# A decode step with attention over a cached K and V: V in tiles of 8 heads in one buffer, K in halves, one softmax per pair

## The chip, the cores and the metric

The kernel runs on one core of a Trainium2 chip. The metric is the device time of one execution in microseconds (us), lower is better. The core has five engines that run side by side and meet at semaphores: PE (TensorE: matrix products, transposes), DVE (VectorE: elementwise work and sums along a row), ACT (ScalarE: activations and copies out of PSUM), POOL (GpSimd: small elementwise work) and SP (SyncE: it only issues transfers here). Transfers are carried by 16 DMA engines; SP's all go through one queue in the order of issue.

## The reference

Eight sequences have one new token each. The token is normalised, projected to 32 query heads of 128, and attends to 4096 cached keys per head; beside it runs a small MLP. The outputs are added.

```python
xn = _layernorm(x, axis=-1)                       # x: 8 x 1 x 640
q = (xn @ wq).reshape(B, 1, 32, 128)              # one query per head
scores = einsum("bhqd,bhkd->bhqk", q, k) * 128 ** -0.5     # k, v: 8 x 32 x 4096 x 128 bf16
p = softmax(scores, axis=-1)
o = einsum("bhqk,bhkd->bhqd", p, v)
return x + o.reshape(B, 1, 4096) @ wo + gelu(_layernorm(xn) @ w1 + b1) @ w2 + b2
```

The K and V caches are 256 MB each, and each of their elements is used once. All weights together are some 15 MB.

## The kernel before, in words

**Tiles.** A tile is 4 heads of one sequence: 4 x 4096 keys, laid out so that partition p holds 128 keys of head p // 32, one after another (32 KB a partition, 4 MB a tile). There are 64 tiles (`NQ`), index i. K and V have two tiles of buffer each (`K_sb`, `V_sb`, slot i % 2).

**Scores.** A tile's keys are split. The first 88 of each partition's 128 are done by DVE in four chunks (`dve_chunk`, L480): multiply by the query, which lies on every partition (`qbc_sb`), add the two halves of the row, sum the rest, into `Sd_sb`. The last 40 (`JP`) are done by PE in five banks of 8: `pe_T` (L437) transposes 8 keys into PSUM, `act_T` (L449) copies them to `KT_sb`, `pe_QK` (L457) multiplies them by the queries of all four heads, so that PSUM (`S_ps`) holds for each key a score against each of the four heads, of which one belongs to it. `act_S` (L470) picks that one with four copies, one for the 32 partitions of each head.

**Softmax.** `dve_max` (L499) finds the maximum over 32 partitions' scores with two 32x32 transposes and makes the bias; `act_exp` (L512) takes the exponential in four instructions of 32 partitions, one a head, each writing its own column of `P_sb` (the other columns stay zero, from one memset at the start) and its row sums. `pe_RS` and `dve_rinv` make the inverse of the sums.

**Output.** `pe_PV` (L535) multiplies V by `P_sb`, key row by key row: 128 products, each with four columns. The zeros keep the heads apart. `act_O` copies the result, `o_norm` (L554) scales it on POOL and spreads it for the last step. After all tiles, `pe_ox` / `cp_ox` turn it, and `fin_wo` multiplies by wo (160 products onto the sum that the MLP began).

**Queries.** `qrep` (POOL), `pe_qbc` and `act_qbc` put the next tile's query on all partitions.

**Order.** Each step is put at a position by `at(pos, fn, ...)` (L686 and on), with tile i at 100 i; the sorted list is then replayed to each engine in that order, so that an engine's order is fixed by hand. PE, DVE and ACT run tiles two by two in a loop of 32 rounds. SP replays its issues in order too: an issue that waits holds up those behind it. `load_k(i)` (L300) waits until tile i-2 has been transposed and multiplied, `load_v(i)` (L310) until PV of tile i-2 is done. The loads of wo come last.

**Start.** The weights of the MLP lie in the second slots of K_sb and V_sb; so K of tile 1 waits for the first MLP product (`mlp1`) and V of tile 1 for the second (`mlp`). The first slots are free at once.

The steps print with the line numbers of the kernel. The profile puts nearly all instructions on L104, where the recorded calls are replayed, so its groups are told apart by tile names; an operation that writes `KT_sb` from `TR_ps` is `act_T`.

Of the kernel before, what the change touches and what calls it, by code (L numbers as in the profile page):

```python
# [13 lines left out]
P = 128  # L14
# [132 lines left out]
def bass_parallel_sum__gqa_block_cached__mixer_channel_mlp__decode_kernel(  # L147
# [17 lines left out]
    HS = 4  # L165
    HP = P // HS
    NKEY = SK * HS // P
    NHQ = H // HS
    NQ = NHQ * B
# [6 lines left out]
    LOOP0, LOOPN = -0.1, 32  # L176
    PAD = 64
    VFIRST = 16
    NR = H * DH // P
    assert NKEY == 128  # L180
    NS = 5

    JP = 40

    def chunks(i):
        jd = NKEY - JP
        n = -(-jd // CHMAX)
        return [(jd * c // n, jd * (c + 1) // n) for c in range(n)]

    bank0 = [0]  # L190
    for i_ in range(NQ):
        bank0.append(bank0[-1] + JP // TPB)
    chunk0 = [0]
    for i_ in range(NQ):
        chunk0.append(chunk0[-1] + len(chunks(i_)))
    V_CUT = {}
    K_CUT = {}
    WO_CUT = (0, 16, 26, 30, NR)
    DQ = DH // NR

# [3 lines left out]
    with ExitStack() as es:  # L204
# [6 lines left out]
        V_sb = sb("V_sb", [P, 2, NKEY, DH], BF)  # L211
# [3 lines left out]
        M_sb = V_sb[:, 1, :, :].rearrange("p j d -> p (j d)")  # L215
        w2_sb = M_sb[:, 0:(FB + 1) * D].rearrange("p (c n) -> p c n", n=D)
        wo_sb = W_sb[:, 0:NR * D].rearrange("p (c n) -> p c n", n=D)
        assert DC * F <= NKEY * DH and (FB + 1) * D <= NKEY * DH and NR * D <= DC * H * DH
# [5 lines left out]
        Sd_sb = sb("Sd_sb", [P, 2, NKEY], F32)  # L224
        P_sb = sb("P_sb", [P, 2, NKEY, HS], BF)
        qT_sb = sb("qT_sb", [P, H, B], BF)
        qrep_sb = sb("qrep_sb", [P, 2, HS, HP], BF)
        qbc_sb = sb("qbc_sb", [P, 2, DH], BF)
        oN_sb = sb("oN_sb", [P, 2, HS], F32)
# [3 lines left out]
        oU_sb = sb("oU_sb", [P, 2, HS], F32)  # L233
# [14 lines left out]
        mq_sb = sb("mq_sb", [P, 1], F32)  # L248
        nsc_sb = sb("nsc_sb", [P, 32], F32)
        mb_sb = sb("mb_sb", [P, 32], F32)  # L250
        NB_sb = sb("NB_sb", [P, 2, 32], F32)
        rs4_sb = sb("rs4_sb", [P, 2, HS], F32)
        ri4_sb = sb("ri4_sb", [P, 2, HS], F32)
# [9 lines left out]
        TRF = TR_ps[:, :, :].bitcast(F32)  # L263
        TRB, SB_, PVB = [_Bank(), _Bank()], [_Bank(), _Bank()], [_Bank(), _Bank()]
        CHB, ACCB = _Bank(), _Bank()
        RS_ps = CH_ps[:, 0:2 * HS].rearrange("p (s h) -> p s h", h=HS)
        QT_ps = CH_ps[:, 64:64 + H * B]
        HT_ps = CH_ps[:, 64:64 + (FB + 1) * B]
        OX_ps = S_ps[:, 0, 0:B * NR].rearrange("p (b c) -> p b c", c=NR)

        pe, dve, act, sp, pool = (_Eng(sem(f"{n}_s")) for n in ("pe", "dve", "act", "sp", "pool"))
        NPIECE = 4
        ld_k = [[_Dma(sem(f"ld_k{s}_{q}")) for q in range(NPIECE)] for s in range(2)]
        ld_v = [[_Dma(sem(f"ld_v{s}_{q}")) for q in range(NPIECE)] for s in range(2)]
# [13 lines left out]
        def cuts(kind, i):  # L288
            c = (K_CUT if kind == "k" else V_CUT).get(i, (0, NKEY))
            return list(zip(c[:-1], c[1:]))  # L290

        def piece_of(kind, i, lo, hi):
            return [tk[(kind, i, q)] for q, (a, b) in enumerate(cuts(kind, i)) if a < hi and b > lo]

        def cache_src(cache, i, lo, hi):
            hq, b = divmod(i, B)
            return cache[b, hq * HS:(hq + 1) * HS].rearrange(
                "h (p j) d -> (h p) j d", j=NKEY)[:, lo:hi, :]

        def load_k(i):  # L300
            s = i % 2
            if i >= 2:
                sp.wait(tk[("kt", i - 2)], tk[("km", i - 2)])
            elif i == 1:
                sp.wait(tk["mlp1"])
            for q, (lo, hi) in enumerate(cuts("k", i)):
                tk[("k", i, q)] = ld_k[s][q].sig(sp.dma_start(
                    K_sb[:, s, lo:hi, :], cache_src(A_k_cache, i, lo, hi)))

        def load_v(i):  # L310
            s = i % 2
            if i >= 1:
                sp.wait(tk[("pv", i - 2)], tk["mlp"])
            for q, (lo, hi) in enumerate(cuts("v", i)):
                tk[("v", i, q)] = ld_v[s][q].sig(sp.dma_start(
                    V_sb[:, s, lo:hi, :], cache_src(A_v_cache, i, lo, hi)))

        def load_mlp():
            tk["w1"] = ld_w1.sig(sp.dma_start(w1_sb, B_w1.rearrange("(p c) f -> p c f", c=DC)))
            tk[("v", -1, 0)] = tk["w2a"] = ld_v[1][0].sig(sp.dma_start(  # L320
                w2_sb[:, 0:FB, :], B_w2[0:FB * P, :].rearrange("(p c) n -> p c n", c=FB)))
            sp.wait(tk["vz"])
            tk["w2b"] = ld_w2b.sig(sp.dma_start(w2_sb[0:FLAST, FB, :], B_w2[FB * P:F, :]))
# [7 lines left out]
        def consts_pool():  # L331
            tk["iota"] = pool.sig(pool.iota(iota_i[:, :], [[1, P]], base=0, channel_multiplier=-1))
            tk["vz"] = pool.sig(pool.memset(M_sb[:, FB * D:NKEY * DH], 0.0))
            pool.memset(Sd_sb[:, 1, :], 0.0)
# [3 lines left out]
            pool.memset(rs4_sb[:, :, :], 0.0)  # L338
# [3 lines left out]
            pool.wait(t)  # L342
            tk["pz"] = pool.sig(pool.memset(P_sb[:, :, :, :].rearrange("p n j h -> p (n j h)"), 0.0))
# [33 lines left out]

        def pe_xT(w):
# [32 lines left out]
        def qrep(i):  # L411
            hq, b = divmod(i % NQ, B)
            s = i % 2
            pool.wait(tk[("q", hq * HS)], tk.get(("qb_pe", i - 2)), tk.get(("qkl", i - 2)))
            tk[("qrep", i)] = pool.sig(pool.tensor_copy(
                qrep_sb[:, s, :, :],
                qT_sb[:, hq * HS:(hq + 1) * HS, b][:, :, None].to_broadcast([P, HS, HP])))

        def pe_qbc(i):
            k = trn[0] % 2  # L420
            trn[0] += 1
            pe.wait(tk[("qrep", i)], tk["id"])
            TRB[k].use(pe)
            tk[("qb_pe", i)] = TRB[k].used(pe, pe.sig(pe.matmul(
                TRF[:, k, 0:DH], qrep_sb[:, i % 2, :, :].rearrange("p h r -> p (h r)"),
                ident_bf[:, :], start=True, stop=True)))
            tk[("qbk", i)] = k

        def act_qbc(i):
            k = tk[("qbk", i)]  # L430
            act.wait(tk.get(("km", i - 2)))
            TRB[k].use(act)
            tk[("qb", i)] = TRB[k].used(act, act.sig(act.activation(
                qbc_sb[:, i % 2, :], TRF[:, k, 0:DH], ACT.Copy)))


        def pe_T(i, t):  # L437
            k = trn[0] % 2
            trn[0] += 1
            s = i % 2  # L440
            j0 = NKEY - JP + t * TPB
            pe.wait(tk["id"], piece_of("k", i, j0, j0 + TPB))
            TRB[k].use(pe)
            for jj in range(TPB):
                last = pe.transpose(TR_ps[:, k, jj * P:(jj + 1) * P], K_sb[:, s, j0 + jj, :], ident_bf[:, :])
            tk[("T", i, t)] = (k, TRB[k].used(pe, pe.sig(last)))
            tk[("kt", i)] = tk[("T", i, t)][1]

        def act_T(i, t):  # L449
            k, _ = tk[("T", i, t)]  # L450
            n = bank0[i] + t
            act.wait(tk.get(("qk", n - NS)))
            TRB[k].use(act)
            tk[("ev", n)] = TRB[k].used(act, act.sig(act.activation(
                KT_sb[:, n % NS, :, :].rearrange("p a b -> p (a b)"), TR_ps[:, k, :], ACT.Copy)))

        def pe_QK(i, t):  # L457
            n = bank0[i] + t
            s = i % 2
            pe.wait(tk[("ev", n)], tk[("qrep", i)])  # L460
            if t == 0:
                SB_[s].use(pe)
            for jj in range(TPB):
                c0 = (t * TPB + jj) * HS
                last = pe.matmul(S_ps[:, s, c0:c0 + HS], KT_sb[:, n % NS, jj, :],
                                 qrep_sb[:, s, :, 0], start=True, stop=True)
            tk[("qk", n)] = SB_[s].used(pe, pe.sig(last))
            tk[("qkl", i)] = tk[("qk", n)]

        def act_S(i):  # L470
            s = i % 2
            if i >= 2:
                act.wait(tk[("exp", i - 2)])
            SB_[s].use(act)
            for h in range(HS):
                r = slice(h * HP, (h + 1) * HP)
                last = act.activation(Sd_sb[r, s, NKEY - JP:NKEY], S_ps[r, s, h:JP * HS:HS], ACT.Copy)
            tk[("s", i)] = SB_[s].used(act, act.sig(last))

        def dve_chunk(i, c):  # L480
            s = i % 2
            lo, hi = chunks(i)[c]
            w = hi - lo
            n = chunk0[i] + c
            dve.wait(piece_of("k", i, lo, hi), tk[("qb", i)], tk.get(("ya", n - 1)))
            tm = dve.sig(dve.tensor_tensor(
                Y_sb[:, 0:w, :], K_sb[:, s, lo:hi, :],
                qbc_sb[:, s, :][:, None, :].to_broadcast([P, w, DH]), ALU.mult))
# [5 lines left out]
            dve.wait(ta, tk.get(("exp", i - 2)))  # L494
            tk[("yr", n)] = dve.sig(dve.tensor_reduce(Sd_sb[:, s, lo:hi], Y2_sb[:, n % 2, 0:w, :],
                                                      AX.X, ALU.add))


        def dve_max(i):  # L499
            s = i % 2  # L500
            dve.wait(tk.get(("s", i)), tk.get(("yr", (chunk0 + [0])[i + 1] - 1)), tk["consts"])
            t = dve.sig(dve.tensor_reduce(mx_sb[:, 0:1], Sd_sb[:, s, :], AX.X, ALU.max))
# [3 lines left out]
            t = dve.sig(dve.tensor_reduce(mq_sb[:, :], mxT_sb[:, :], AX.X, ALU.max))  # L506
            dve.wait(t)
            t = dve.sig(dve.tensor_scalar(mb_sb[:, :], nsc_sb[:, :], mq_sb[:, 0:1], None, ALU.mult))
            dve.wait(t, tk.get(("exp", i - 2)))
            tk[("nb", i)] = dve.sig(dve.transpose(NB_sb[:, s, :], mb_sb[:, :]))  # L510

        def act_exp(i):  # L512
            s = i % 2
            act.wait(tk[("nb", i)], tk.get(("pv", i - 2)), tk.get(("rs", i - 2)), tk["pz"])
            for h in range(HS):
                r = slice(h * HP, (h + 1) * HP)
# [326 lines left out]
```

## Time and profile before

| | |
|---|---|
| median of 3 runs | 1288.07 us (1287.66 to 1288.30) |
| the profiled execution, its time | 1287.84 us |
| its span | 1286.0 us |
| busy: DVE, PE, ACT, POOL | 1127.0, 665.9, 585.4, 116.5 us |
| bytes read from HBM | 551.80 MB, 429 GB/s over the span |
| granted PE clock, mean | 0.562 |

The profile is of one execution. The span runs from its first to its last instruction; the time that the runs are compared by is 1.84 us longer here. A group row of the profile reads: line, engine, operation, written tile <- read tiles, shapes, count, then busy time and mean ns of one, then the idle time of the engine ahead of these instructions and what ended it. A timeline row reads: start, length, engine, operation; in brackets the idle time ahead and who ended it. The page cuts the span into 40 slices of 32 us; a 9 is a slice with 90% or more of busy time. The chain follows the last instruction back, at each step to what released it. PEld is PE's weight load, which overlaps its products.

### The profile page before, as it was taken

What the parts mean: (1) busy time and instruction counts of PE and PEld (TensorE: products, weight loads), DVE (VectorE), ACT (ScalarE), POOL (GpSimd) and SP (SyncE); (2) the same over time, 40 slices, a digit from 0 to 9 for tenths busy, and PEclk for the clock granted to TensorE, in tenths of its full rate; (3) what the DMA queues carried; (4) which work ended last, traced back from release to release, by engine and by line L of the source; (5) the groups of instructions that cost most, each with busy time, mean ns of one, the idle gap of its engine ahead of it and who ended that gap; (6) DMA issues with size and microseconds to landing.
All of it is one profiled execution on the core that took longest, in us unless ns stands there. A gap on an engine that the chain in (4) does not pass through costs nothing.

```text
span 1286.0 us, 33792 instructions
## 1 busy us (share of the span) xinstructions
PE 665.9 (52%) x14139; PEld 602.5 (47%) x14139; DVE 1127.0 (88%) x1186; ACT 585.4 (46%) x1264; POOL 116.5 (9%) x207
## 2 busy tenths in 40 slices
PE   4635446446464544554644544554554555555455
PEld 4535445445454544544544544544444444444445
DVE  2889889889899998988988989989889889889885
ACT  1525445445463543543544544544544534535433
POOL 2010100110111010000000000000000000000000
PEclk9955555555555555555555555555555656555555
DMA  9999999999999999999999999999999999999998
GB/s 397 434 428 434 430 432 432 430 434 429 435 428 434 428 436 428 435 428 434 430 433 430 433 431 433 431 432 431 432 432 431 432 431 433 429 434 430 434 428 367
DMA packets 19603, 551.99 MB, mean 429 GB/s; under 512 B 2236, under 2 KB 2309, under 8 KB 2566
## 3 DMA queue, kind: packets, MB, share of 16 engines
q1 hardware_dynamic: 19570, 551.80, 99.8%
q8 instruction: 8, 0.13, 0.0%
q14 instruction: 5, 0.04, 0.0%
q10 hardware_dynamic: 20, 0.02, 0.0%
HBM read 551.80 MB, written 0.01 MB: 429 GB/s over the span
## 4 chain that ended last, share of the span: by engine, by line
DMA 61%; DVE 25%; issue 12%; PE 1%; POOL 1%; ACT 0%; DVEq 0%; SPq 0%; POOLq 0%; ACTq 0%
DMA K_sb<-in_A_k_cache_dram 58%; DVE Y_sb L104 24%; DMA W_sb<-in_A_wo_dram 3%; DVE Sd_sb L104 1%; POOL V_sb L104 1%; DVE ri_sb L104 0%; PE PV_ps L104 0%; PE TR_ps L104 0%; DVEq L102 0%; SPq L104 0%; ACT KT_sb L104 0%; ACT P_sb L104 0%; DVE mx_sb L104 0%; DVE mb_sb L104 0%; DVE mxT_sb L104 0%
## 5 line engine op out<-in xcount | busy, mean ns | idle before, releaser
L104 ACT ACTIVATE KT_sb<-TR_ps 128x1024 bf16<-128x1024 bf16 x320 | 318.5, 1022 | 432.9 <-PE TR_ps L104 430.8
L104 PE MATMUL TR_ps<-ident_bf,K_sb 128*128 128x128 bf16 x2560 | 302.7, 301 | 381.5 <-DMA K_sb<-in_A_k_cache_dram 381.5
L104 DVE TENSOR_TENSOR Y_sb<-K_sb,qbc_sb 128x2816 bf16<-128x2816 bf16 x256 | 412.7, 1612 | 90.6 <-DMA K_sb<-in_A_k_cache_dram 90.6
L104 PEld LDWEIGHTS TR_ps<-ident_bf,K_sb 128*128 128x128 bf16 x2560 | 242.7, 138 | 386.6 <-DMA K_sb<-in_A_k_cache_dram 386.6
L104 DVE TENSOR_REDUCE Sd_sb<-Y_sb 128x22 f32<-128x1408 bf16 x256 | 414.7, 1620 | 8.7
L104 DVE TENSOR_TENSOR Y_sb<-Y_sb 128x1408 bf16<-128x1408 bf16 x256 | 228.3, 892 | 8.7
L104 PEld LDWEIGHTS PV_ps<-P_sb,V_sb 128*128 128x128 bf16 x8320 | 232.1, 105 | 4.3 <-DMA V_sb<-in_A_v_cache_dram 4.3
L104 PE MATMUL PV_ps<-P_sb,V_sb 128*128 128x4 bf16 x8320 | 231.3, 166 | 3.0 <-DMA V_sb<-in_A_v_cache_dram 3.0
L104 PE MATMUL S_ps<-qrep_sb,KT_sb 128*128 128x4 bf16 x2560 | 121.6, 171 | 73.4 <-ACT KT_sb L104 69.5
L104 PEld LDWEIGHTS S_ps<-qrep_sb,KT_sb 128*128 128x128 bf16 x2560 | 100.1, 105 | 123.1 <-ACT KT_sb L104 119.5
L104 ACT ACTIVATE P_sb<-Sd_sb,NB_sb 32x128 bf16<-32x128 f32 x260 | 149.5, 575 | 6.0 <-DVE NB_sb L104 1.4
L104 POOL TENSOR_TENSOR oN_sb<-oU_sb,ri_sb 128x4 f32<-128x4 f32 x64 | 37.1, 580 | 1136.8 <-ACT oU_sb L104 1045.5
L104 PE MATMUL CH_ps<-rs_sb,ones_f 128*128 128x4 f32 x130 | 38.0, 363 | 138.3 <-ACT P_sb L104 138.3
L104 ACT ACTIVATE oU_sb<-PV_ps 128x4 f32<-128x4 f32 x64 | 11.1, 174 | 208.0 <-PE PV_ps L104 208.0
L104 PEld LDWEIGHTS CH_ps<-rs_sb,ones_f 128*128 128x128 f32 x130 | 32.6, 312 | 143.9 <-issue 86.7
L104 ACT ACTIVATION_READ_ACCUMULATOR P_sb<-Sd_sb,NB_sb 32x1 f32 x260 | 64.7, 249 | 0.0
L104 POOL TENSOR_TENSOR oM_sb<-oN_sb,mask_sb 128x16 bf16<-128x16 f32 x64 | 55.1, 862 | 5.0
L104 ACT ACT_TABLE_LOAD x34 | 43.6, 1283 | 14.9 <-issue 6.2
L104 ACT ACTIVATE Sd_sb<-S_ps 32x40 f32<-32x40 f32 x256 | 48.9, 191 | 2.2
L104 DVE TENSOR_REDUCE mx_sb<-Sd_sb 128x1 f32<-128x128 f32 x65 | 18.6, 286 | 10.7 <-ACT hT_sb L104 8.5
L104 ACT ACTIVATE qbc_sb<-TR_ps 128x128 bf16<-128x128 f32 x65 | 18.0, 278 | 9.0 <-PE TR_ps L104 7.2
L104 POOL COPY qrep_sb<-qT_sb 128x128 bf16<-128x128 bf16 x65 | 18.5, 285 | 7.3 <-DVE qT_sb L104 7.3
(65 smaller groups left out, 152.4 us busy)
## 6 DMA issues: line engine op xcount, KB each, us to landing
K_sb<-in_A_k_cache_dram SPq DMA_DIRECT2D x64, 4096.0 KB, 24.7
V_sb<-in_A_v_cache_dram SPq DMA_DIRECT2D x64, 4096.0 KB, 34.1
W_sb<-in_A_wq_dram SPq DMA_DIRECT2D x1, 5120.0 KB, 15.3
W_sb<-in_A_wo_dram SPq DMA_DIRECT2D x1, 2560.0 KB, 31.2
K_sb<-in_B_w_dram SPq DMA_DIRECT2D x1, 2160.0 KB, 20.0
V_sb<-in_B_w_dram SPq DMA_DIRECT2D x1, 2080.0 KB, 25.4
W_sb<-in_A_wo_dram SPq DMA_DIRECT2D x1, 1600.0 KB, 34.5
W_sb<-in_A_wo_dram SPq DMA_DIRECT2D x1, 640.0 KB, 35.6
```

Source lines behind the costliest of these rows:

```text
L104: inst = getattr(e, name)(*a, **k)
```

## The change: what it does

- A tile of V is 8 heads of one sequence (`HS` = 8, a pair, index g, 32 of them): 64 KB a partition, 256 keys, 16 partitions a head, 8 MB. `V_sb` is one buffer of that size in place of two of half the size. `load_v(g)` waits for PV of pair g-1 and for the MLP's second product, also for g = 0, since the MLP's weights now lie in this one buffer. V of pair 30 is loaded in two halves, the second one issued when the first has landed.
- K is loaded in halves of the pair's keys, index i = 2g and 2g+1, each into one of the two slots of `K_sb`: 32 KB of each partition's 64.
- Of a half's 128 keys, 64 (before 40) go to PE, in 8 banks, and 64 to DVE, in three chunks (21, 21 and 22 keys). `KT_sb` has 4 slots, not 5. QK has 8 columns.
- `act_S` goes. `dve_S`, on DVE, multiplies S_ps by a 0/1 mask of the partition's head and sums over the 8 heads.
- One softmax a pair, over 256 scores a partition: `dve_max` for 8 heads, one exponential over all 128 partitions into `E_sb`, then `dve_ex` on DVE: the row sums and E_sb times the mask, into `P_sb` with 8 columns. PV has 256 products of 8 columns. E_sb, P_sb, Sd_sb, qbc_sb and the small tiles have one slot, not two.
- The masks are made once at the start (`masks`). The query's transpose uses the PSUM bank of the row sums, not a transpose bank.
- In the order of PE, row sums and PV of pair g-1 stand right ahead of the first half of pair g; on DVE the softmax of pair g-1 stands ahead of the chunks of pair g, and dve_S behind the chunks of its half. The loop still has 32 rounds, one pair each.
- SP's order is K(2g), K(2g+1), V(g), and at the end K61, V30 first half, K62, V30 second half, K63, V31, wo.

```diff
-    HS = 4
+    HS = 8
     HP = P // HS
-    NKEY = SK * HS // P
-    NHQ = H // HS
-    NQ = NHQ * B
+    NJ = SK * HS // P
+    NKEY = NJ // 2
+    NG = H // HS * B
+    NQ = 2 * NG
...
-    NS = 5
-    JP = 40
+    NS = 4
+    JP = 64
+    JD = NKEY - JP
...
-        V_sb = sb("V_sb", [P, 2, NKEY, DH], BF)
+        V_sb = sb("V_sb", [P, NJ, DH], BF)
...
         def load_k(i):
-            s = i % 2
+            g, s = divmod(i, 2)
             if i >= 2:
                 sp.wait(tk[("kt", i - 2)], tk[("km", i - 2)])
             elif i == 1:
                 sp.wait(tk["mlp1"])
...
+            tk[("k", i)] = ld_k[s].sig(sp.dma_start(
+                K_sb[:, s, :, :], cache_src(A_k_cache, g, s * NKEY, (s + 1) * NKEY)))
...
+        def load_v(g, half=None):
+            if half != 1:
+                sp.wait(tk[("pv", g - 1)], tk["mlp"])
+            else:
+                sp.wait(tk[("vh", g)])
+            lo, hi = (0, NJ) if half is None else (half * NKEY, (half + 1) * NKEY)
+            d = ld_vh if half == 0 else ld_v
+            tk[("vh" if half == 0 else "v", g)] = d.sig(sp.dma_start(
+                V_sb[:, lo:hi, :], cache_src(A_v_cache, g, lo, hi)))
...
-        def act_S(i):
...
+        def dve_S(i):
             s = i % 2
+            SB_[s].use(dve)
+            dve.wait(tk["mask8"], tk.get(("s", i - 1)))
+            t = SB_[s].used(dve, dve.sig(dve.tensor_tensor(
+                SM_sb[:, :, :], S_ps[:, s, 0:JP * HS].rearrange("p (j h) -> p j h", h=HS),
+                mask8f[:, :][:, None, :].to_broadcast([P, JP, HS]), ALU.mult)))
+            dve.wait(t)
+            tk[("s", i)] = dve.sig(dve.tensor_reduce(
+                Sd_sb[:, s * NKEY + JD:(s + 1) * NKEY], SM_sb[:, :, :], AX.X, ALU.add))
...
-        def act_exp(i):
...
+        def act_E(g):
+            act.wait(tk[("nb", g)], tk.get(("ex", g - 1)))
+            tk[("E", g)] = act.sig(act.activation(E_sb[:, :], Sd_sb[:, :], ACT.Exp, bias=NB_sb[:, 0:1],
+                                                  scale=SCALE, accum_out=rs1_sb[:, 0:1]))
+
+        def dve_ex(g):
+            dve.wait(tk[("E", g)], tk.get(("pv", g - 1)), tk.get(("rs", g - 1)), tk["mask8"])
+            tk[("r8", g)] = dve.sig(dve.tensor_scalar(rs8_sb[:, :], mask8f[:, :], rs1_sb[:, 0:1], None, ALU.mult))
+            tk[("ex", g)] = dve.sig(dve.tensor_tensor(
+                P_sb[:, :, :], E_sb[:, :][:, :, None].to_broadcast([P, NJ, HS]),
+                mask8b[:, :][:, None, :].to_broadcast([P, NJ, HS]), ALU.mult))
...
+        def pe_PV(g):
+            PVB[0].use(pe)
+            pe.wait(tk[("ex", g)], tk[("v", g)], tk["vz2"])
+            for j in range(NJ):
+                last = pe.matmul(PV_ps[:, 0, 0:HS], V_sb[:, j, :], P_sb[:, j, :], start=(j == 0), stop=(j == NJ - 1))
+            tk[("pv", g)] = PVB[0].used(pe, pe.sig(last))
...
+        for g in range(-1, NG):
+            o = (2 * g + 2) * Q
+            at(o, dve_max, g)
+            at(o + 2, act_E, g)
+            at(o + 3, dve_ex, g)
+            at(o + 4, pe_RS, g)
+            at(o + 5, pe_PV, g)
+            if g < NG - 1:
+                at(o + 5.5, act_O, g)
+            at(o + 45, dve_rinv, g)
+            at(o + 46, o_norm, g)
         for i in range(NQ):
+            g, s = divmod(i, 2)
             o = i * Q
...
             if i >= 2:
-                at(o - 90 if i > VFIRST else o - 79, load_k, i)
-            if i >= 1:
-                at(o + 20, load_v, i)
...
+                at(o - 95, load_k, i)
+            if s == 0:
+                at(o + 5.6, load_v, g, *((0,) if g == NG - 2 else ()))
+            elif g == NG - 2:
+                at(o + 6, load_v, g, 1)
+            tw = 35.0 / NB_
+            for t in range(NB_):
+                at(o + 6 + tw * t, pe_T, i, t)
+                at(o + 6 + tw * (t + 0.4), act_T, i, t)
+                at(o + 6 + tw * (t + 1.5), pe_QK, i, t)
+            for c in range(NCH):
+                at(o + 10 + 75.0 * c / NCH, dve_chunk, i, c)
+            at(o + 86, dve_S, i)
+            if s == 1:
+                at(o + 82, qrep, g + 1)
+                at(o + 83, pe_qbc, g + 1)
+                at(o + 84, act_qbc, g + 1)
```

The loop over pairs also holds a dummy pair -1, whose PV is taken with the MLP's weights in V_sb and is not used.

## The prediction

> **What bounds the kernel now.** I read the page's slices and queue table first, then the chain, then the timeline of the end, then the timeline of one tile, then the groups.
>
> ```profile
> DMA  9999999999999999999999999999999999999998
> q1 hardware_dynamic: 19570, 551.80, 99.8%
> DMA 61%; DVE 25%; issue 12%; PE 1%; POOL 1%; ACT 0%; DVEq 0%; SPq 0%; POOLq 0%; ACTq 0%
> 1207.19 0.33 SPq L104 DMA_DIRECT2D K_sb<-in_A_k_cache_dram  x1
> 1226.61 0.33 SPq L104 DMA_DIRECT2D K_sb<-in_A_k_cache_dram  x1
> ```
>
> The 16 DMA engines are busy in every slice, and one queue holds 99.8% of their time. Two K issues stand 19.42 us apart, and in that time one K and one V tile (8.39 MB) move: 9.71 us a tile, 432 GB/s. DVE's 88% is cover, not the bound. Only what leaves the queue empty, or follows its last byte, can cost time. The end:
>
> ```profile
> 1251.36 1.62 DVE L104 TENSOR_TENSOR Y_sb<-K_sb,qbc_sb 128x2816 bf16<-128x2816 bf16 x1 [1.51 <-DMA K_sb<-in_A_k_cache_dram]
> 1255.48 1.61 DVE L104 TENSOR_TENSOR Y_sb<-K_sb,qbc_sb 128x2816 bf16<-128x2816 bf16 x1
> ...
> 1268.07 0.29 DVE L104 TENSOR_REDUCE mx_sb<-Sd_sb 128x1 f32<-128x128 f32 x1
> 1271.15 0.57 ACT L104 ACTIVATE P_sb<-Sd_sb,NB_sb 32x128 bf16<-32x128 f32 x1
> 1272.23 3.55 PE L104 MATMUL PV_ps<-P_sb,V_sb 128*128 128x4 bf16 x128
> 1277.00 2.28 PE L104 MATMUL ACC_ps<-oX_sb,W_sb 128*128 128x8 bf16 x80 [0.54 <-DMA W_sb<-in_A_wo_dram]
> 1280.75 2.75 PE L104 MATMUL ACC_ps<-oX_sb,W_sb 128*128 128x8 bf16 x80 [1.48 <-DMA W_sb<-in_A_wo_dram]
> 1283.54 0.20 DVE L104 CAST resT_sb<-ACC_ps 128x40 bf16<-128x40 f32 x1 [6.74 <-PE ACC_ps L104]
> ```
>
> The last K tile lands at 1251.36; behind it two V tiles and wo still move. The computation of that tile is done at 1275.8 (PV), the last products wait for wo (1.48 us), and end at 1283.50. So today the end hangs on the last bytes, with some 1.5 us of computing to spare. One tile on PE:
>
> ```profile
> 1231.95 1.89 PE L104 MATMUL TR_ps<-ident_bf,K_sb 128*128 128x128 bf16 x16 [6.14 <-DMA K_sb<-in_A_k_cache_dram]
> 1234.10 0.38 PE L104 MATMUL S_ps<-qrep_sb,KT_sb 128*128 128x4 bf16 x8 [0.26 <-ACT KT_sb L104]
> 1238.83 0.38 PE L104 MATMUL S_ps<-qrep_sb,KT_sb 128*128 128x4 bf16 x8 [0.80 <-ACT KT_sb L104]
> 1241.88 3.43 PE PV_ps L104 x128
> ```
>
> First QK 2.15 us after the first transpose, the fifth 4.73 us later: 1.18 us a bank of 8 keys. PV is 26.8 ns a product.
>
> **The change part by part**
>
> *Bytes.* Removed: 64 V transfers of 4 MB. Added: 31 of 8 MB and two halves. K keeps 64 of 4 MB. Cost 0 if the rate stays. No row has 64 KB pieces. The nearest are the 32 KB ones (432 GB/s for 1185 us); the farthest is wo, in pieces of 20 to 2.5 KB (10 KB mean), which moved at 368 GB/s from 1271 to 1283, about 405 without its idle last microsecond. A fixed cost a piece fitted through both is 0.037 us, and would make a V pair 19.42 - 0.29 us: -9.3 us over 32. I take 0, by the nearer row; -9.3 stays for the range.
>
> *The V buffer.* The V load of pair g now waits on SP for PV of pair g-1, and the K loads of the next pair stand behind it on SP. The order is K(2g), K(2g+1), V(g); K62 below is half 62, V30 the V of pair 30. Count from K(2g)'s landing. If PV(g-1) ends at x, V(g) is issued then; the queue holds K(2g+1) until 9.71. An issue needs at most 1.7 us to take effect (x_sb is issued at 0.74, its reader starts at 2.46), so nothing is lost while x is under 8.0. K(2g+2) waits for K(2g)'s readers (about 10.5) and is wanted at 29.1: free.
>
> *The cycle.* x stays put only if one round of computing takes under a pair's 38.84 us, because PE's order is PV(g-1), K(2g), K(2g+1), DVE's is softmax, half, dve_S, half, dve_S, and dve_S of the first half waits for PE. The round: PV 256 x 26.8 ns = 6.86; transposes and QK of 8 banks 2.15 + 7 x 1.18 + 0.38 = 10.79; dve_S, two passes over 512 f32, each the 128-element maximum's 0.29 plus 384 elements at 0.96 a ns = 0.69, together 1.42 with a gap; three chunks 12.0 (22 keys take 1255.48 - 1251.36 = 4.12, 21 keys 3.95); dve_S 1.42; maximum chain 1.27 (1268.07 to 1269.34) + 0.13 for 256 scores = 1.41; one exponential 0.58 + 0.11 = 0.69 (in place of four); the 0/1 product of 2048 elements, 2.29, with the row sums' scaling 0.2; five hand-overs of 0.05. Sum 37.3 us, 1.5 under the pair. So x falls by 1.5 a pair from its start (PV(0) ends about 4.4 after K2 lands) to about -0.2, and the transfers hide all of it.
>
> The 0/1 product is the open price. TENSOR_TENSOR Y_sb of 1408 bf16 takes 0.892 us, TENSOR_REDUCE of 1408 1.620. By the first, 2048 cost 1.22, by the second 2.29. I take the second: E_sb repeats each element eight times, while the fast row has neighbours in both operands. The Trainium skill, "VectorE: DVE Perf Modes", What auto-detection actually checks, gives the double rate only where every operand has step one, which agrees; by it the product costs 2.29, by the plain row the sum is 1.1 less. No row shows a repeated bf16 operand.
>
> *DVE and ACT relief.* DVE loses a chunk in four (64 keys instead of 88), ACT the 32-row copies of S and three quarters of the exponentials. Worth 0: both lie under the transfers.
>
> *Start.* V(0) waits for mlp and the dummy PV(-1) (256 products now): maximum from 31.3, exponential 33.4, product 36.0, PV 42.9. K1, issued at 30.9, moves from 37.0 to 46.7: 3.8 to spare, 1.7 needed. Cost 0. POOL's 6.8 us memset of V_sb is off SP's path, but the queue was full there: 0. The masks run while DVE waits for wq: 0.
>
> *The end.* Here the cover is gone. After K63 the same bytes follow (V31, wo), so K63 lands at 1251.36 again. But the order is V30 first half, K62, V30 second half, K63, V31, wo, and PV(30) needs both halves: it can't start before 1251.36 - 9.71 = 1241.65. Its 256 products stand on PE in front of all of K62. From there: PV 1248.56; K62 on PE 1259.35; dve_S 1260.82 (DVE had finished K62's chunks and idles); K63's chunks 1272.82; dve_S 1274.24; maximum 1275.65; exponential 1276.44; product 1278.93; PV(31) 1285.98. From PV to the first wo product 1.2 us as before (1275.8 to 1277.0): 1287.2. 160 products at 26.7 ns, 4.4: 1291.6, against 1283.50. **+8.1 us.** V31, issued at 1248.6, is in time; wo has landed 4 us before it is wanted.
>
> The clock enters here: K62's stretch is 10.8 us. In the windows of one microsecond, the granted clock was 0.50 through all of the stretch from 1232, but went to 0.81 and 1.00 from 1216, four microseconds into the stretch from 1212. I price it at half clock; at full clock ACT's 1.02 us a bank limits, 1.6 less. The Trainium skill, "TensorE: Matmul & The Clock Gate", Part 1, releases the clock after a busy window of about 3.4 us; one of the two stretches agrees. By it the last 4 us run fast, 3 to 4 banks at 0.15 less, and the end costs 7.6, not 8.1.
>
> **Sum.** 0 + 0 + 8.1: the profiled execution took 1287.84 (span 1286.0 and 1.84 around it), 0.23 below the median 1288.07; forecast 1287.84 + 8.1 + 0.23 = 1296.2 us. Its own range: 1.1 (product) and 1.6 (clock) below, 1.5 for slower hand-overs above: 1293 to 1298.
>
> **Rivals**
>
> *Longer pieces move faster (other side).* Place: the V transfers. It decides from 0.17 us a tile: 32 x 0.17 = 5.5 leaves +2.6, 0.2%, about what a measurement here can tell. At 0.29 a tile the time is 1296.2 - 9.3 = 1286.9, no change. For it: wo's slower rate. Against: 32 KB rows are already steady at 432, and wo's end is unclear. The skill's "DMA: Bandwidth & Descriptors", Where 436 GB/s comes from, puts the ceiling at 435.2 GB/s; an estimate by it is 0.14 a tile, 4.6 us in all, 1291.6: slower still.
>
> *The round is longer than the pair.* It decides from +1.5 us. If the 0/1 product took two cycles an element (+2.1), the round is 39.5, V(g) is late once x passes 8.0, and 31 pairs cost 0.6 each, less 3.6 of slack, and 2.1 + 1 more at the end: 1296 + 15 + 3 = 1314. For: three new DVE passes with no row of their own; against: passes with rows of their own fill 32 of 37.3.
>
> *The new source pattern is slower.* K halves are 32 KB pieces every 64 KB. At wo's 405 GB/s each K half takes 0.65 more: 64 x 0.65 = 42, 1338. Nothing in the profile speaks for it; nothing shows the pattern.
>
> **How the numbers follow.** Forecast 0.64, faster pieces 0.18, longer round 0.12, slower pattern 0.06. Left out of 1287 to 1304: the slow pattern 0.06, most of the longer round 0.09, the far end of the faster pieces 0.05. Within 0.2% (1285.5 to 1290.6) lies the faster pieces' main part, 0.10; if the end is also cheaper by product and clock, faster, 0.08; the rest, 0.82, is slower.
>
> **What would show it.** After: DMA at 9 in all slices but the last, K issues in pairs every 38.8 us; SP's wait for PV short of any gap. The 0/1 product near 2.3 us, dve_S's passes near 0.69. At the end the wo products no longer wait for wo but follow oX_sb, near 1287, and PE idles before PV(30) for the second V half. Wrong if the landings are closer than 38.8 us a pair, if an empty slice shows in the middle, or if wo still ends last.

## The result, and the profile after

The changed kernel takes 1295.46 us (median of 4 runs, 1295.21 to 1295.79) against 1288.09 before: 1.0058 times, with an interval of 1.0040 to 1.0075. It is slower by 7.4 us; the forecast was 1296.2. The profiled execution took 1295.58 us, its span is 1293.8 us.

The page of the kernel after: DMA's slices, two rows of the queue table, the chain.

```profile
DMA  9999999999999999999999999999999999999996
q1 hardware_dynamic: 15106, 551.80, 99.0%
q8 instruction: 10, 0.16, 0.1%
DMA 63%; PE 14%; DVE 9%; ACT 8%; issue 6%; DVEq 0%; ACTq 0%; POOL 0%; SPq 0%
```

The transfer engines are busy in every slice but the last, as before. DVE's share of the chain falls from 25% to 9%, and PE and ACT come in with 14% and 8%. 14% of the span are 181 us, far more than the end has: the chain passes transposes, copies and PV in the loop too, where the queue is full all the same. What the end goes through is read from its timeline, below. The row q8, transfers of instructions, is quoted because it matters below.

One round of the kernel after, in the timeline; the last line is the first chunk of half 2g, released by its keys' landing, and the V issue stands on SP.

```profile
650.57 2.29 DVE L104 TENSOR_TENSOR P_sb<-E_sb,mask8b 128x2048 bf16<-128x2048 bf16 x1
652.99 6.99 PE L104 MATMUL PV_ps<-P_sb,V_sb 128*128 128x8 bf16 x256 [1.60 <-DVE P_sb L104]
660.00 0.33 SPq L104 DMA_DIRECT2D V_sb<-in_A_v_cache_dram  x1
660.21 1.56 DVE L104 TENSOR_TENSOR Y_sb<-K_sb,qbc_sb 128x2688 bf16<-128x2688 bf16 x1 [7.35 <-DMA K_sb<-in_A_k_cache_dram]
```

PV ends 0.2 us ahead of the next keys: the x of the prediction is -0.2, and the next V is issued 8 us before it would be late by the prediction's count. The 0/1 product takes 2.29 us. The end:

```profile
1241.95 6.99 PE L104 MATMUL PV_ps<-P_sb,V_sb 128*128 128x8 bf16 x256 [9.05 <-DMA V_sb<-in_A_v_cache_dram]
1248.80 1.87 PE L104 MATMUL TR_ps<-ident_bf,K_sb 128*128 128x128 bf16 x16
1248.97 0.33 SPq L104 DMA_DIRECT2D V_sb<-in_A_v_cache_dram  x1
...
1258.47 0.69 DVE L104 TENSOR_TENSOR SM_sb<-S_ps,mask8f 128x512 f32<-128x512 f32 x1 [12.03 <-PE S_ps L104]
1259.80 1.55 DVE L104 TENSOR_TENSOR Y_sb<-K_sb,qbc_sb 128x2688 bf16<-128x2688 bf16 x1
...
1271.81 0.68 DVE L104 TENSOR_TENSOR SM_sb<-S_ps,mask8f 128x512 f32<-128x512 f32 x1
1275.41 2.28 DVE L104 TENSOR_TENSOR P_sb<-E_sb,mask8b 128x2048 bf16<-128x2048 bf16 x1
1277.75 6.64 PE L104 MATMUL PV_ps<-P_sb,V_sb 128*128 128x8 bf16 x243 [1.60 <-DVE P_sb L104]
1285.08 0.51 PE L104 MATMUL PV_ps<-P_sb,V_sb 128*128 128x8 bf16 x13 [0.68 <-issue]
1286.68 4.55 PE L104 MATMUL ACC_ps<-oX_sb,W_sb 128*128 128x8 bf16 x160 [0.39 <-DVE oX_sb L104]
1291.26 0.20 DVE L104 CAST resT_sb<-ACC_ps 128x40 bf16<-128x40 f32 x1 [4.64 <-PE ACC_ps L104]
```

PE stands 9 us for the second half of V30; half 62 follows behind PV(30); DVE, done with its own part of half 62, stands 12 us for PE's part, and only then starts on half 63. The last products follow oX_sb, not wo. They end at 1291.23, where the kernel before ended them at 1283.50.

**Where the 7.7 us lie** (profiled executions, 1287.84 and 1295.58). The fifth tile in the queue is the first one whose landing both traces show at a waiting reader: 75.97 before, 78.48 after (its line stands in the section on the start), **+2.5**. In the kernel before:

```profile
75.97 1.62 DVE L104 TENSOR_TENSOR Y_sb<-K_sb,qbc_sb 128x2816 bf16<-128x2816 bf16 x1 [3.23 <-DMA K_sb<-in_A_k_cache_dram]
```

From there the kernel before moves 121 tiles of 4 MB up to half 63's keys at 1251.36, 9.714 us a tile; the kernel after moves 120 up to V30's second half at 1241.95, 9.696 a tile, so over 120 tiles **-2.2**. These two all but cancel: V30's second half lands 0.3 later than the 1241.65 counted from the kernel before. The rest, **+7.4**, is the computing behind that landing.

### The profile page after: what moved, and what is told of

It reads as the page before. It is cut to its first block, busy times and chain, and to the rows that moved or that the text cites. A ratio compares the mean times of both kernels' runs of the same rounds, so it can differ in the third digit from the quotient of the medians.

```text
span 1293.8 us, 38899 instructions
## 1 busy us (share of the span) xinstructions
PE 779.9 (60%) x17243; PEld 684.2 (53%) x17243; DVE 977.3 (76%) x1000; ACT 581.4 (45%) x682; POOL 97.6 (8%) x111
## 4 chain that ended last, share of the span: by engine, by line
DMA 63%; PE 14%; DVE 9%; ACT 8%; issue 6%; DVEq 0%; ACTq 0%; POOL 0%; SPq 0%
DMA K_sb<-in_A_k_cache_dram 58%; ACT KT_sb L104 7%; DVE Y_sb L104 7%; PE TR_ps L104 6%; PE PV_ps L104 4%; DMA V_sb<-in_A_v_cache_dram 3%; PE S_ps L104 3%; DMA W_sb<-in_A_wq_dram 1%; DVE P_sb L104 1%; PE CH_ps L104 1%; DVE SM_sb L104 1%; DVE Sd_sb L104 0%; PE ACC_ps L104 0%; DVE mx_sb L104 0%; ACT E_sb L104 0%
## 5 line engine op out<-in xcount | busy, mean ns | idle before, releaser
L104 ACT ACTIVATE KT_sb<-TR_ps 128x1024 bf16<-128x1024 bf16 x512 | 501.4, 1022 | 100.4 <-PE TR_ps L104 97.8
L104 DVE TENSOR_TENSOR Y_sb<-K_sb,qbc_sb 128x2688 bf16<-128x2688 bf16 (+1 forms) x192 | 300.6, 1566 | 217.5 <-DMA K_sb<-in_A_k_cache_dram 217.5
L104 PE MATMUL TR_ps<-ident_bf,K_sb 128*128 128x128 bf16 x4096 | 383.9, 255 | 11.0 <-DMA K_sb<-in_A_k_cache_dram 9.8
L104 PEld LDWEIGHTS TR_ps<-ident_bf,K_sb 128*128 128x128 bf16 x4096 | 301.1, 115 | 14.3 <-DMA K_sb<-in_A_k_cache_dram 12.1
L104 DVE TENSOR_REDUCE Sd_sb<-Y_sb 128x21 f32<-128x1344 bf16 (+1 forms) x192 | 302.5, 1576 | 6.6
L104 PE MATMUL PV_ps<-P_sb,V_sb 128*128 128x8 bf16 x8448 | 230.9, 168 | 63.9 <-DVE P_sb L104 51.3
L104 PE MATMUL S_ps<-qrep_sb,KT_sb 128*128 128x8 bf16 x4096 | 193.8, 177 | 110.6 <-ACT KT_sb L104 98.2
L104 PEld LDWEIGHTS S_ps<-qrep_sb,KT_sb 128*128 128x128 bf16 x4096 | 147.3, 100 | 190.4 <-ACT KT_sb L104 187.2
L104 DVE TENSOR_TENSOR Y_sb<-Y_sb 128x1344 bf16<-128x1344 bf16 (+1 forms) x192 | 167.5, 873 | 6.6
L104 DVE TENSOR_TENSOR P_sb<-E_sb,mask8b 128x2048 bf16<-128x2048 bf16 x33 | 75.4, 2284 | 0.0
```

The source lines that it names most:

```text
L104: inst = getattr(e, name)(*a, **k)
```

## Experiments

All times are medians; the kernel before took 1288.16 to 1288.28 on the same chips.

### V30 in one piece

```diff
-                at(o + 5.6, load_v, g, *((0,) if g == NG - 2 else ()))
-            elif g == NG - 2:
-                at(o + 6, load_v, g, 1)
+                at(o + 5.6, load_v, g)
```

> Edit: V of pair 30 is loaded in one piece, as the other pairs are; SP's end order becomes K61, V30, K62, K63, V31, wo. My theory (the end is a chain of computing that starts when V30's second half lands, at 1241.95 in the changed kernel's profile, because PV(30) stands ahead of K62 on PE): V30 lands about 1232, PV(30) follows the 0/1 product and is over by 1241.5, half 62 is handled from its landing near 1242, so PV(31) ends near 1280.4 in place of 1285.6 and the last wo product near 1286. The median falls by about 5 us, to 1290.5. Rival (the split is harmless, what lengthened the end is the slower softmax and the longer PV alone): PV(31) ends where it did, 1295.5 within 1 us.

Measured: 1292.57 us (1292.07 to 1293.82), 1.0033 times before: 2.9 less than the changed kernel, not 5. The end of this kernel in the timeline (the profiled execution took 1293.82):

```profile
1236.37 6.99 PE L104 MATMUL PV_ps<-P_sb,V_sb 128*128 128x8 bf16 x256 [1.60 <-DVE P_sb L104]
1243.72 1.56 DVE L104 TENSOR_TENSOR Y_sb<-K_sb,qbc_sb 128x2688 bf16<-128x2688 bf16 x1 [7.48 <-DMA K_sb<-in_A_k_cache_dram]
1255.81 0.68 DVE L104 TENSOR_TENSOR SM_sb<-S_ps,mask8f 128x512 f32<-128x512 f32 x1
1257.12 1.55 DVE L104 TENSOR_TENSOR Y_sb<-K_sb,qbc_sb 128x2688 bf16<-128x2688 bf16 x1
1269.12 0.68 DVE L104 TENSOR_TENSOR SM_sb<-S_ps,mask8f 128x512 f32<-128x512 f32 x1
```

PV(30) no longer waits for V, and half 62 starts on PE with its landing, 5 us earlier than in the changed kernel. But now DVE has both last halves in front of it from 1243.72 on and works through them without a gap: 25.4 us to the last dve_S, which comes only 2.7 us earlier; 0.9 of that goes into a gap in the last PV (1.59 us of issue, 0.68 in the changed kernel). So the split of V30 is what holds PV(30) up, and what was late next is DVE. DVE is not all that is missing from the 5 us: in this execution, the longest of the six, half 60's keys land 1.9 us later than in the changed kernel (1204.94 against 1203.08), and this was lost before half 6 (157.93 against 156.04), in rounds that the edit leaves alone.

### The last round ahead of its end: written out, and PV(30) behind half 62

The loop gets 31 rounds and the last one is written behind it: first in the same order (a control), then with PV(30), its copy and its scaling behind half 62, and V31 issued after.

```diff
-    LOOP0, LOOPN = -0.1, NG
+    LOOP0, LOOPN = -0.1, NG - 1
...
+            d = 45 if g == NG - 2 else 0
-            at(o + 5, pe_PV, g)
+            at(o + 5 + d, pe_PV, g)
...
+                at(o + 5.6 + (45 if g == NG - 1 else 0), load_v, g, *((0,) if g == NG - 2 else ()))
```

> Edit: the last of the 32 rounds stands behind the loop instead of in it; the order on every engine is the same. It is the control for the next run, which needs a last round of its own. Both theories: 1295.5 within 1 us. If code loading costs, up to 3 us more (PE stalled 2.9 us in the first round's PV of the changed kernel with nothing in the profile that it waited for).

> Edit: last round behind the loop; in it PV(30), the copy of its result and its scaling are moved behind the QK of half 62, and V31 is issued behind K63 as before but after that PV. Split of V30 kept. My theory: PE handles half 62 from its landing near 1232 while V30's second half is still on its way, PV(30) runs from about 1243 to 1250, K63 goes through DVE as soon as it lands (1251.7), PV(31) starts when V31 lands (about 1272) and ends near 1279; the end hangs on wo again, which lands 0 to 2 us later than in the changed kernel because V31 is issued at 1250, 1 us later. Median 1289 to 1290.5. Rival (the split and PE's order are harmless): 1295.5 within 1 us.

Measured: the control 1297.82 (1296.58 to 1298.12), 2.4 slower than the loop; the moved PV 1298.13, no gain over the control in the median. Its five executions fall into two groups, 1298.13 to 1298.49 three times and 1294.82 and 1295.13; the trace is of the 1298.13. The miss is the most useful run of the study. PV(30) in the control, timeline:

```profile
1242.23 6.81 PE L104 MATMUL PV_ps<-P_sb,V_sb 128*128 128x8 bf16 x250 [9.14 <-DMA V_sb<-in_A_v_cache_dram]
1250.91 0.32 PE L104 MATMUL PV_ps<-P_sb,V_sb 128*128 128x8 bf16 x6 [1.87 <-issue]
```

The same 256 products ran without a break in the changed kernel, with the same transfers on their way. Here PE waits 1.87 us for nothing that the profile names. The page of the control counts four more transfers of instructions, and two of them lie between 1246 and 1254, where the changed kernel has none:

```profile
q8 instruction: 14, 0.23, 0.1%
```

Ten such transfers serve the whole kernel with its 32 looped rounds; every copy of a round that is written out adds some. That PE stands while its code comes is followed up in the next section. With the moved PV, timeline:

```profile
1243.34 3.34 PE L104 MATMUL PV_ps<-P_sb,V_sb 128*128 128x8 bf16 x122
1249.90 3.78 PE L104 MATMUL PV_ps<-P_sb,V_sb 128*128 128x8 bf16 x134 [3.22 <-issue]
1253.72 0.33 SPq L104 DMA_DIRECT2D V_sb<-in_A_v_cache_dram  x1
1267.58 2.28 DVE L104 TENSOR_TENSOR P_sb<-E_sb,mask8b 128x2048 bf16<-128x2048 bf16 x1
1275.93 3.07 PE L104 MATMUL PV_ps<-P_sb,V_sb 128*128 128x8 bf16 x110 [7.61 <-DMA V_sb<-in_A_v_cache_dram]
1281.72 3.56 PE L104 MATMUL PV_ps<-P_sb,V_sb 128*128 128x8 bf16 x128 [2.72 <-issue]
1287.64 0.62 PE L104 MATMUL PV_ps<-P_sb,V_sb 128*128 128x8 bf16 x18 [2.36 <-issue]
```

The computing did move: the last 0/1 product starts at 1267.58, not 1275.41, 7.8 us earlier. But PV(30) has a hole of 3.2 us, V31 is issued 4.75 us later and lands at 1275.9, and the last PV has two more holes. Together 8.3 us; an estimate without them, from these rows, is V31 issued at 1250.5, landed at 1272.7, PV(31) done at 1279.7. The last load of wo, which landed at 1289.1, would land at 1285.9 then, so the last products would end near 1286.2 in place of 1293.8, a time near 1290.5. That is the upper end of what was expected. It was not reached in any execution.

### What the code waits for

The last kernel once more, without the four loads of wo:

```diff
-            at(o - 60 + q, load_wo, q)
+            pass
...
-            pe.wait(tk[("oX", B - 1)], tk[("oX", B)], tk[("wo", q)])
+            pe.wait(tk[("oX", B - 1)], tk[("oX", B)])
```

> The kernel of the moved PV(30) once more, with the four loads of wo left out (the 160 last products are made with what lies in that buffer, so the output isn't the reference's). There the last PV, run for the first time, was held by PE's issue for 2.72 us after 110 products and for 2.36 us after 128 more, while wo was on its way. If these waits are the time that a block of code takes to come whatever else moves, they stay: 2 to 3 us each, time 1297 to 1298.5. If the code stands behind wo's bytes on the transfer engines, which have nothing to move here from V31's landing at 1275.9, they shrink to under 1 us each and the time falls by 3.5 to 5 us, to 1293 to 1294.6. The wait of 3.2 us in PV(30), where K63 is on its way, stays in both cases.

Measured: 1294.5 us in a single run, 3.6 less. Timeline of this kernel:

```profile
1249.04 3.57 PE L104 MATMUL PV_ps<-P_sb,V_sb 128*128 128x8 bf16 x128 [2.65 <-issue]
1253.87 0.33 PE L104 MATMUL PV_ps<-P_sb,V_sb 128*128 128x8 bf16 x6 [1.26 <-issue]
1277.66 6.97 PE L104 MATMUL PV_ps<-P_sb,V_sb 128*128 128x8 bf16 x256 [9.11 <-DMA V_sb<-in_A_v_cache_dram]
```

With no wo behind V31 the last PV has no hole here; PV(30), where K63 is on its way, has two (2.65 and 1.26 us). The time falls into the range of the second reading, but this doesn't show that wo's bytes made the code late: it is a single execution, and two of the five executions with wo, 1294.82 and 1295.13, took hardly longer.

What the traces do show is when the code came. There are 28 holes of over 0.25 us in the PVs of the traces after the change, and each of them ends 1.2 to 1.6 us after a transfer of 16 KB on the instruction queue (q8) has ended, 2.2 to 2.6 us after that transfer started. So PE does stand for its code, and how long depends on how early the transfer starts. In the last PV it started 3.8 us after the first product without the dummy pair (next section), and there was no hole; 4.9 us in the changed kernel, and the hole was 0.68; 6.0 us with the other order of DVE (below), and it was 1.78. Without wo a transfer started at 1270.82, ahead of the last PV; with wo the corresponding one started at 1279.49, 3.6 us into it. A start held up by data ahead of it would fit this; it is argued, not shown.

### The start

The dummy pair is left out, and the first round is written ahead of the loop, which has 31.

```diff
-    LOOP0, LOOPN = -0.1, NG
+    LOOP0, LOOPN = 1.9, NG - 1
...
-        for g in range(-1, NG):
+        for g in range(0, NG):
```

> Edit: the dummy pair -1 is left out (it computes nothing that is used), the first round stands ahead of the loop, and the rest of V_sb is not cleared; V0 then waits only for the MLP's second product. My theory: in the changed kernel V0 was issued at 45.5, too late for the queue, and K2 landed at 78.5, 2.4 us later than the bytes in front of it allow (37.3 + 29.1 + 9.7); with V0 issued near 33 this gap goes and all behind it moves up: K2 lands near 76.1, median 1293.1. Rival (the prediction's step 'start costs 0': the queue was full): K2 lands at 78.5 as before and the median stays at 1295.5 within 1 us.

Measured: 1294.69 us (1294.62 to 1294.78), 0.8 less. The start of the changed kernel and then of this one, in their timelines:

```profile
35.45 3.79 PE L104 MATMUL PV_ps<-P_sb,V_sb 128*128 128x8 bf16 x136 [1.60 <-DVE P_sb L104]
42.09 3.37 PE L104 MATMUL PV_ps<-P_sb,V_sb 128*128 128x8 bf16 x120 [2.86 <-issue]
45.49 0.33 SPq L104 DMA_DIRECT2D V_sb<-in_A_v_cache_dram  x1
78.48 1.56 DVE L104 TENSOR_TENSOR Y_sb<-K_sb,qbc_sb 128x2688 bf16<-128x2688 bf16 x1 [2.56 <-DMA K_sb<-in_A_k_cache_dram]
```

```profile
69.00 3.76 PE L104 MATMUL PV_ps<-P_sb,V_sb 128*128 128x8 bf16 x135 [1.60 <-DVE P_sb L104]
75.18 3.39 PE L104 MATMUL PV_ps<-P_sb,V_sb 128*128 128x8 bf16 x121 [2.42 <-issue]
76.24 1.56 DVE L104 TENSOR_TENSOR Y_sb<-K_sb,qbc_sb 128x2688 bf16<-128x2688 bf16 x1 [7.38 <-DMA K_sb<-in_A_k_cache_dram]
```

The first PV of the changed kernel has the hole too, and V0 goes out at 45.49, not 42.9. Without the dummy pair half 2's keys come 2.24 us earlier. Half 4's come 2.24 earlier too (115.02 against 117.26), half 6's only 0.87 (155.17 against 156.04), half 60's 0.93 (1202.15 against 1203.08), and in the time 0.8 is left. The first PV has its hole here too, 2.42 us, but that isn't what takes the gain back: half 4's keys follow half 2's in 38.78 us, and the loss falls into the next pair, where PV(1) at 110.35 has no hole. What took 1.4 us there stays open. The last PV, whose first run this is as well, has no hole:

```profile
1277.71 6.99 PE L104 MATMUL PV_ps<-P_sb,V_sb 128*128 128x8 bf16 x256 [1.60 <-DVE P_sb L104]
```

The start and the moved PV together:

> Edit: no dummy pair, and PV(30) behind the QK of half 62; first and last round outside the loop. My theory: the two gains add, since one is an empty queue at the start and the other a chain of computing behind the last transfers: -2.4 and -5 to -6.5, median 1287 to 1288, as fast as the kernel before or up to 1 us faster. Rival (the two repair the same us, an earlier queue only uncovers the end's computing): not under 1289.5.

Measured: 1297.17 us (1296.89 to 1298.21), for the same reason: three PVs with holes.

### How near the round is to the pair

The 0/1 product is made twice, and three times, in each round; the output is the same.

```diff
+            for r_ in range(2):
+                if r_:
+                    dve.wait(tk[("ex", g)])
```

> Edit: the 0/1 product into P_sb is done twice in each pair (same result), which lengthens the round of computing by one product, 2.3 us. My theory (steady state is hidden only while the round is shorter than a pair's transfers): the changed kernel's round, from its rows, is 36.9 us against 38.78 a pair; with 39.2 it is 0.4 too long, x creeps up from pair to pair until V is issued late, and the pairs then follow at 39.2: about 30 x 0.4 less 1 to 3.5 of slack, plus 2.3 once at the end: 1295.5 + 11 to 14 = 1306 to 1310. Rival (DVE idles 217 us for K, so 75 us more on DVE are simply hidden): 1295.5 + 2.3 = 1298.

> Edit: the 0/1 product is done three times in each pair. My theory: round 36.9 + 4.6 = 41.5 us, 2.7 over the pair; K issues in steady state 41.5 apart; 31 x 2.7 less 1 to 3.5 of slack plus 4.6 at the end: 1295.5 + 85 = 1380 within 5 us. Rival (hidden by DVE's idle time, which is 7 us a pair): K issues 38.8 apart, 1295.5 + 4.6 = 1300.

Measured: 1300.87 us twice, 1370.63 three times; both stay under the 1306 and the 1375 that the theory asked for at least. The knee is there, but lies further out than the prediction put it. Three times, two rounds in the timeline:

```profile
650.41 6.94 DVE L104 TENSOR_TENSOR P_sb<-E_sb,mask8b 128x2048 bf16<-128x2048 bf16 x3
664.50 0.33 SPq L104 DMA_DIRECT2D V_sb<-in_A_v_cache_dram  x1
691.08 6.94 DVE L104 TENSOR_TENSOR P_sb<-E_sb,mask8b 128x2048 bf16<-128x2048 bf16 x3
705.17 0.33 SPq L104 DMA_DIRECT2D V_sb<-in_A_v_cache_dram  x1
```

From V1's issue at 90.89 to V29's at 1237.96 a round takes 40.97 us; less the two added products (6.94 - 2.29 = 4.65) that is 36.3. Twice: from 86.59 (V1) to 1207.97 (V30) it takes 38.67, less 2.32 is 36.35. Both give a round of 36.3 us in the place of 37.3, 2.5 under the pair's 38.78. So doubling it does not reach the bound, and its 5.4 us lie at the two ends: half 2's keys come 2.8 later, half 60's 2.9, the rest is behind them.

### What the longer pieces brought

V stays one transfer of 8 MB, but its buffer has a gap in the middle of each partition, so the pieces are 32 KB.

```diff
-        V_sb = sb("V_sb", [P, NJ, DH], BF)
+        V_sb = sb("V_sb", [P, 2, NKEY * DH + 64], BF)
```

> Edit: 128 bytes lie between the two halves of V_sb in each partition, so that a V transfer of 8 MB is still one transfer, but is written in pieces of 32 KB, not 64. It tells apart why a pair of transfers takes 38.78 us now and 38.84 before. If the gain is in the pieces (a fixed cost for each): the period goes back to 38.84 and the median up by about 2 us, to 1297.5. If it is in the number of transfers (64 V transfers became 33): period 38.78, median 1295.5 within 0.7.

Measured: 1296.78 us (1296.34 to 1297.59), 1.3 more. From half 4 to half 60, 28 pairs, a pair takes 38.809 us (117.16 to 1203.81) against 38.779 with 64 KB (117.26 to 1203.08) and 38.856 before; the pair from half 2 to 4 took 39.22 here against 38.78 and is left out. In the nine other kernels with 64 KB pieces whose period is set by the queue (all but the one with three products) a pair takes 38.777 to 38.785 from half 20 to 60, so 0.030 is clear of the noise. Of 0.077 us a pair, then, some 0.030 comes with the length of the pieces and 0.047 with something else in the change: the number of transfers is one candidate, the places from which K's halves are read another, and no run tells these apart. Each is small; the medians alone would not show it, the periods do.

### The order of DVE at the end

dve_S of the even half goes behind the odd half's chunks, in every round, so the loop stays as it is.

```diff
-            at(o + 86, dve_S, i)
+            at(o + (162 if s == 0 else 86), dve_S, i)
```

> The order of DVE alone is changed, in every round: the even half's masked PE scores (dve_S(2g)) are taken behind the three product chunks of the odd half and no longer ahead of them; PE, ACT and SP keep their order. Theory of the end (in the last pair DVE stands 12.03 us for PE's scores of half 62 while half 63's keys have been there for most of it, so its chunks, 12 us, begin only at 1259.8 and set dve_S(63) at 1271.8, where PE had done half 63 at 1267.1): the chunks begin with half 63's landing near 1251.5, dve_S(63) goes by PE at about 1267.3, 4.5 us earlier, V31 (landing near 1271.0) and wo (near 1282) are just in time, and all ends 4.5 us earlier: time 1291.0, range 1290 to 1292. Rival (the end goes by the bytes: wo's last landing, or V31's): no more than 1.5 us gained, 1294 to 1295.5. If the order costs the steady rounds something (odd chunks wait for a later landing), above 1296.

Measured: 1293.14 us (1292.83 to 1294.26), 1.0040 times before (1.0027 to 1.0054), 2.3 less than the changed kernel. Timeline:

```profile
1251.55 1.56 DVE L104 TENSOR_TENSOR Y_sb<-K_sb,qbc_sb 128x2688 bf16<-128x2688 bf16 x1 [5.05 <-DMA K_sb<-in_A_k_cache_dram]
1268.06 0.69 DVE L104 TENSOR_TENSOR SM_sb<-S_ps,mask8f 128x512 f32<-128x512 f32 x1 [3.10 <-PE S_ps L104]
1274.02 6.64 PE L104 MATMUL PV_ps<-P_sb,V_sb 128*128 128x8 bf16 x243 [1.60 <-DVE P_sb L104]
1282.44 0.51 PE L104 MATMUL PV_ps<-P_sb,V_sb 128*128 128x8 bf16 x13 [1.78 <-issue]
```

DVE starts half 63 with its landing and now waits for PE, as expected: the last dve_S comes 3.75 us earlier. The last PV gives 1.1 of that back in a longer hole (1.78 us, not 0.68); that more of wo's bytes are on their way there could be the reason, but is not shown.

### Three edits together

The order of DVE as above, no dummy pair, and the last 0/1 product in two halves with PV beginning behind the first.

```diff
+            cuts = (0, NKEY, NJ) if g == NG - 1 else (0, NJ)
...
+                if g == NG - 1 and j == NKEY:
+                    pe.wait(tk[("ex", g)])
```

> Three edits to the changed kernel together: the order of DVE as in the run before it (-4.5 by theory), the unused pair -1 left out and the first round written ahead of the loop (-0.8 measured), and the last pair's 0/1 product made in two halves of the keys, PV beginning behind the first (2.28 us become 1.14 ahead of PV: -1.1). If the gains lie one behind the other on the chain of the end, 1295.5 - 6.4 = 1289.1, range 1288 to 1290.5, still no faster than the kernel before at 1288.1; V31's landing (near 1270) would then be within 1 to 2 us of the bound. Rival (bytes or first execution of code at the end take over): 1291 or above.

Measured: 1290.78 us (11 runs, 1289.79 to 1292.06), 1.0020 times before (1.0011 to 1.0029). 4.7 of the 7.4 us are recovered, not 6.4; 1290.78 lies between the theory's range and the rival's 1291. In the traced execution, 1292.01, the last PV has a hole of 2.35 us:

```profile
1281.60 0.53 PE L104 MATMUL PV_ps<-P_sb,V_sb 128*128 128x8 bf16 x14 [2.35 <-issue]
```

No version of the study is faster than the kernel before.

## Why the prediction was right or wrong, point by point

- **The end, +8.1:** right in its place and its order, and nearly in its size. V30's second half came at 1241.95 (predicted 1241.65), the last dve_S at 1271.81 (1272.82), PV(31) ended at 1285.6 (1286.0), the products at 1291.23 (1291.6). Behind the landing 7.4 us were added. Half 62's stretch on PE took 9.6 us, not 10.79; a hole of 0.7 in the last PV gave part back. The sum has 4.4 us for the last 160 products, where its own 26.7 ns each makes 4.27; they took 4.55.
- **The clock** was priced at half through that stretch. In windows of one microsecond it was 0.50 to 1251 and 1.00 from 1252, 3 us into the transposes but 10 us after PE had begun to work without a break; in the round above PE works from 653, and it is 0.50 to 668. The Trainium skill, "TensorE: Matmul & The Clock Gate", Part 1, releases the clock after a busy window of about 3.4 us. Counted from PE's first product, the trace differs by 6 us and more; counted from the transposes, this end agrees, and the round (8 us) and the end of the kernel without the dummy pair (transposes from 1247.87, 0.50 to 1256) do not.
- **Start, cost 0:** the term that was mis-sized most: +2.5. The prediction moved K1 to 46.7 with 3.8 us to spare and counted PV(-1) as 256 products without a hole. V0 went out 2.6 late, and the keys of the fifth tile came 2.5 late. The hole of 2.86 us made V0 late, and the queue ran dry: by the starts and lengths of the single transfers in the trace, the 16 engines worked 0.60 of the time from 44 to 48, some 1.6 us lost, where the kernel before and the one without the dummy pair kept them at work all the time. Where the other 0.9 us went is not shown: without the dummy pair 2.24 went away, but hole and pair went together.
- **Bytes, cost 0:** mis-sized by -2.2, 0.077 us a pair, of the same sign as the rival but a quarter of its 0.29. The rival "longer pieces move faster" had the sign, not the size: the run with 32 KB pieces gives the pieces 0.030 us of the 0.077. The Trainium skill, "DMA: Bandwidth & Descriptors", Where 436 GB/s comes from, gives a ceiling of 435.2 GB/s; a pair of 16.78 MB in 38.779 us is 432.6, under it, and the trace agrees.
- That the start and the bytes cancelled to 0.3 is luck; the forecast's 0.7 us of error hides two errors of more than 2.
- **The cycle:** the sign was right, 37.3 was 36.3, and x fell to -0.2 as predicted. The rival "the round is longer than the pair" was less near than its 0.12: the run with the product twice has the two added microseconds that it feared, and its round, 38.67, still fits.
- **The 0/1 product** was 2.28 us, **dve_S** 0.68 and 0.69: the rows chosen were the right ones.
- **DVE and ACT relief, 0:** right. DVE's busy time fell from 1127 to 977 us, and the steady rounds, which go by the queue, gained no more than the 0.077 us a pair.
- **The slow source pattern:** no sign of it.

## What to carry to other kernels

Where the transfers bound a kernel, a larger tile is worth its 0.08 us a pair in the loop and costs at the ends, where the last tile's whole chain of computing lies open: work that end out by itself, landing by landing, and ask which engine is the next to be late. A wait that is free in every round of a loop (DVE's for PE's scores, here) can be the one that sets the end. A round that is written out behind the loop to mend this runs new code, and code that comes late can cost as much as the mend brings; an order that can be changed inside the loop is the safer edit.

## What the runs showed of the hardware that was not expected

- PV of 256 products, 7.0 us in a loop's later rounds, had holes of 0.4 to 3.3 us each, up to 5.6 us in one PV, where its code ran for the first time: at the start, in a written-out round, behind the loop. The transfers of instructions rise from 10 to 12, 14 and 16 as rounds are written out. Each of the 28 holes ended 2.2 to 2.6 us after such a transfer had started. Not every first run has a hole: the last PV without the dummy pair had none, with wo on its way until about 1282, and its transfer had started early in it (3.8 us, against 4.9 and 6.0 where there was one). What sets the start of the transfer stays open.
- PE's granted clock stayed at 0.50 through 7 us of products of 8 columns, with PE busy the whole time, and rose only after transposes had followed. It is not that such products take it away: at the start it was 1.00 through PV(-1) (35.5 to 45.5), the hole included.
